# Tagging all routed rows with one copy, and SyncE's order written out in a mixture-of-experts layer

## The chip, the cores and the metric

The kernel runs on one core of a Trainium2 chip. The metric is the time of one execution on the device in microseconds (us); of the kernel before there are three runs.

## The reference

Attention over clusters, a dense layer, and a noisy top-2 mixture of eight experts, on 2 x 768 = 1536 tokens of 512 numbers. All is fp32. The last part, which the change is in:

```python
logits = x @ w_gate                                   # 1536 x 8
noisy_logits = logits + np.log1p(np.exp(x @ w_noise)) * noise
top2 = np.argpartition(-noisy_logits, 2, axis=1)[:, :2]
top2_w = softmax(noisy_logits at top2)
for e in range(8):
    for k in range(2):
        mask = top2[:, k] == e
        h = np.maximum(x[mask] @ w1[e], 0.0)          # 512 -> 1024
        out[mask] += top2_w[mask, k, None] * (h @ w2[e])
```

The attention masks each query's scores to the keys of its own cluster; the dense layer is 512 -> 2048 -> 512 with h * sigmoid(1.702 h) between.

## The kernel before

Every fp32 product is made of three matmuls of a high and a low part (hi x hi, hi x lo, lo x hi), so weights and activations exist as pairs: ACT casts the high part (`weights_hi`, `hh`, `xT` at index 0), DVE or POOL subtracts the low one (`weights_lo`, `hl`, `xT` at index 1).

The program has three stretches. Attention lasts to about 440 us. The dense layer works on the two batches b = 0 and b = 1 in turn; between its steps a hook routes b = 0 and starts loading the first expert. `middle` (576 to 632 us) routes b = 1 beside the first halves of experts 0 and 1; its instructions stand in order of a table of times, WIN, and the engines keep that order. `moe2` runs what is left, and `rest` holds loops for tokens beyond the capacities.

**Routing.** For each batch the 768 tokens stand in NB = 6 row blocks of 128 tokens, 512 numbers and 4 tag numbers each (R, ROW = 516). DVE works out each token's two experts, weights and slots. `route_scatter(R, j)` copies the tags of block j into R (L1041) and sends the block's rows to its two slots in the DRAM tensor xs, by two indirect DMAs of POOL (L1043): twelve per batch. `route_end` (L1050 and on), after b = 1 only, ranks experts 2 to 7 by their number of tokens, largest first (`rank`, result ord and ordi), and fills a small table tab for `rest` (`table`), with nr, the number of rounds.

**The experts.** Experts 0 and 1 take 480 rows each, in two halves of 240 (`gather_half`, tile Xh; the second half needs b = 1's scatters). The other six follow in order of size with capacities CAPS of 108 x 4, 104 x 4, 102 x 4, 100 x 4, 98 x 4 and 128 x 3 rows; slot e below is the e-th expert in that order, from 2 to 7. `gather(e)` loads a slot's rows as tile X (L1158). Xh and X share one buffer (tag R of the pool `rows`), so a gather must wait until PE has transposed the whole of the tile before. PE transposes 128 columns at a time (`xpose_part`, L1229) into xT, then runs FFN1 in eight blocks fb (L1325) and FFN2 (L1348 for the halves, L1378 for the slots). After each FFN1 block ACT makes hh (L1333) and DVE hl (L1334).

**Weights.** An expert's weights come in eight parts of 512 KB, in the order ORDER = (0, 4, 1, 5, 2, 6, 3, 7), by SP's DMA queue into staging tiles (`weights_load`, L1117 and L1119), cast by ACT (L1126), with the low part by DVE or POOL (L1130). Even experts use the tiles wA and wg, odd ones wB and wx, so one expert's weights load while the other's are in use.

In `moe2`, `load(e)` issues for slot e a register load of the expert's number from ordi, the eight parts and then the gather; `turn(e)` transposes; `load(e + 1)` stands ahead of slot e's FFN in the program. The order of each engine in `moe2` is made by a scheduler from the dependencies and its own estimate of times; the program's order is only its input. SP's queue and ACT's and PE's instructions so stand in an order that the code doesn't show.

Of the kernel before, what the change touches and what calls it, by code (L numbers as in the profile page):

```python
# [8 lines left out]
F32 = mybir.dt.float32  # L9
# [604 lines left out]
class Moe:  # L614
# [38 lines left out]

    def init_piece(self, i):
# [383 lines left out]

    def route_scatter(self, R, j):
        nc = self.nc  # L1040
        nc.vector.tensor_copy(R[j][:, DM:ROW], self.rmeta[:, j, :])  # L1041
# [8 lines left out]
    def route_end(self):  # L1050
        v, end = self.nc.vector, self.rtot[:, NB, 0:2]
        over = self.rtile("over", 2)
        v.tensor_scalar(over, end, float(-MAIN), 0.0, op0=OP.add, op1=OP.max)
        v.scalar_tensor_tensor(end, over, float(MAIN), self.over[:, 0], op0=OP.add, op1=OP.add)
        self.rank(self.rtot[:, NB, :])
        self.table(self.rtot[:, NB, :])

    def rank(self, total):

        c, v, n = self.const, self.nc.vector, E - 2  # L1060
        key, pos = c.tile([128, n], F32, name="key"), c.tile([128, n], F32, name="rpl")
        big = self.rtile("big", n, n)
        self.ord, self.cap = c.tile([128, n], F32, name="ord"), c.tile([128, E], F32, name="cap")
        self.ordi = c.tile([128, n], I32, name="ordi")
        v.scalar_tensor_tensor(key, total[:, 2:], float(E), self.ie[:, 2:], op0=OP.mult, op1=OP.subtract)
        row = lambda a: a[:, None, :].to_broadcast([128, n, n])
        col = lambda a: a.rearrange("p (n o) -> p n o", o=1).to_broadcast([128, n, n])
        v.tensor_tensor(big, row(key), col(key), op=OP.is_gt)
        v.tensor_reduce(pos.rearrange("p (n o) -> p n o", o=1), big, axis=AX.X, op=OP.add)
        v.tensor_tensor(big, row(pos), col(self.ie[:, :n]), op=OP.is_equal)  # L1070
        at = self.rtile("at", n, n)
        v.tensor_tensor(at, big, row(self.ie[:, 2:]), op=OP.mult)
        v.tensor_reduce(self.ord.rearrange("p (n o) -> p n o", o=1), at, axis=AX.X, op=OP.add)
        v.tensor_copy(self.ordi, self.ord)
        caps = c.tile([128, n], F32, name="caps")
        for r, (cp, ck) in enumerate(CAPS):
            v.memset(caps[:, r:r + 1], float(cp * ck))
        v.tensor_tensor(at, big, col(caps), op=OP.mult)
        v.memset(self.cap[:, :2], float(CAP))
        v.tensor_reduce(self.cap[:, 2:].rearrange("p (n o) -> p n o", o=1), at.rearrange("p r n -> p n r"),  # L1080
                        axis=AX.X, op=OP.add)

    def table(self, total):
        nc, v = self.nc, self.nc.vector
        tb = self.const.tile([128, ROUNDS, E, 4], F32, name="tb")
        v.memset(tb, 0.0)
        for r in range(1, ROUNDS):
            o = BASE + CMIN + (r - 1) * CAP
            v.tensor_scalar_add(tb[:, r, :, 0], total, float(-o))
            v.tensor_scalar(tb[:, r, :, 1], self.ie, float(REG), float(o), op0=OP.mult, op1=OP.add)  # L1090
            v.tensor_copy(tb[:, r, :, 2], self.ie)
        v.tensor_scalar_add(tb[:, 1, :, 3], self.cap, float(-CMIN))
        nc.sync.dma_start(self.tab.rearrange("(o r) n -> o (r n)", o=1), tb[0:1].rearrange("p r e n -> p (r e n)"))
        mx = self.const.tile([128, 1 + ROUNDS], F32, name="mx")
# [54 lines left out]
    def weights(self, e, par):  # L1149
        we = [w[bass.ds(e, 1)].rearrange("o k n -> (o k) n") for w in (self.w1, self.w2)]  # L1150
        W = [None] * 8
        for s in ORDER:
            W[s] = self.weights_part(e, par, s, we)
# [416 lines left out]
```

## Time and profile before

| | us |
|---|---|
| runs before | 936.96, 939.82, 941.28 |
| median of them | 939.82 |
| profiled execution | 941.51 |
| its span | 939.6 |

The span is the time from the first to the last instruction in the trace of the profiled execution; 1.9 us of its time lie around it. Positions below count from the span's start. TensorE's granted clock was 0.972 of the full clock over the span. A page line gives an engine's busy time, its share of the span and its number of instructions; a timeline line gives start, length, engine, line and operation, output <- inputs, and in brackets for how long the engine had been idle before it and what released it. SPq is the DMA queue of SP.

### The profile page before, as it was taken

Reading aid. Unit: us, or ns where it says so; the run is one execution under the profiler, and the core shown is the slowest. Engines: PE = TensorE matmul, PEld = TensorE weight load, DVE = VectorE, ACT = ScalarE, POOL = GpSimd, SP = SyncE. Lnnn points to the kernel's source line nnn. Section 1 sums busy time; section 2 is a strip of 40 time slices with the busy share of each in tenths; the row PEclk is TensorE's granted clock in tenths of the full one; section 3 lists DMA queues with packets and bytes.
Section 4 is the critical chain, followed back from the end, with each engine's and each line's share of the span. In section 5 each row is a group of like instructions: output and inputs, shape, how many; then the busy total and the mean of one; then the engine's idle time right before and its main releaser. Section 6 shows DMA issues by size and latency. Waiting matters only on the chain. (4 is left out here: it accounts for less than half of the span.)

```text
span 939.6 us, 14934 instructions
## 1 busy us (share of the span) xinstructions
PE 887.8 (94%) x5277; PEld 812.0 (86%) x5277; DVE 592.7 (63%) x1190; ACT 489.6 (52%) x1021; POOL 374.8 (40%) x398
## 2 busy tenths in 40 slices
PE   6999999999898999999999999899999899999993
PEld 4898989899887888888998979888889799999992
DVE  3889898998884667675447643836564445555231
ACT  2788888888794556554445433414444243432210
POOL 3134443454455988880000601562341334342121
PEclk8999999999898999999999999899999899999997
DMA  8756675677331344311111331274774737552120
GB/s 212 192 145 184 165 202 137 177 186 206 110 127 33 111 135 119 118 42 61 44 28 32 144 88 46 90 243 121 242 208 117 182 109 210 171 178 68 33 66 35
DMA packets 77532, 120.14 MB, mean 128 GB/s; under 512 B 9858, under 2 KB 55939, under 8 KB 76941
## 3 DMA queue, kind: packets, MB, share of 16 engines
q1 hardware_dynamic: 69997, 100.98, 37.5%
q0 software_dynamic: 7456, 18.16, 6.1%
q8 instruction: 43, 0.70, 0.3%
q14 instruction: 36, 0.29, 0.1%
HBM read 72.85 MB, written 23.76 MB: 103 GB/s over the span
## 5 line engine op out<-in xcount | busy, mean ns | idle before, releaser
L434 DVE TENSOR_TENSOR PTl<-ps_pt,PTh 128x384 fp32r<-128x384 f32 x192 | 98.8, 549 | 11.5 <-ACT PTh L429 10.4
L429 ACT ACTIVATE PTh<-ps_pt 128x384 fp32r<-128x384 f32 x192 | 87.9, 497 | 29.1 <-PE ps_pt L419 28.0
L402 DVE TENSOR_REDUCE nm<-ps_s 128x1 f32<-128x768 f32 x96 | 91.2, 950 | 15.1 <-PE ps_s L397 14.8
L419 PE MATMUL ps_pt<-ident,P 128*128 128x128 f32 x576 | 88.2, 277 | 3.8 <-DVE PTl L434 3.5
L410 ACT ACTIVATE P<-ps_s,nm 128x768 f32<-128x768 f32 x96 | 87.3, 910 | 4.9 <-DVE nm L402 4.9
L1333 ACT ACTIVATE hh<-bank 128x240 fp32r<-128x240 f32 (+6 forms) x80 | 35.2, 446 | 90.7 <-PE bank L1325 84.7
L1325 PE MATMUL bank<-xT,wB 128*128 128x240 f32 (+3 forms) x480 | 82.1, 319 | 0.0
L419 PEld LDWEIGHTS ps_pt<-ident,P 128*128 128x128 f32 x576 | 68.4, 141 | 13.8 <-DVE PTl L434 10.8
L1325 PEld LDWEIGHTS bank<-xT,wB 128*128 128x128 f32 x480 | 76.7, 189 | 2.5 <-DVE hl L1334 0.3
L1130 POOL TENSOR_TENSOR wA<-stg,wA 128x512 fp32r<-128x512 f32 x16 | 20.7, 1296 | 139.1 <-DVE wol L714 66.7
L822 PE MATMUL bank<-woh,gh 128*128 128x512 f32 x192 | 76.2, 397 | 0.0
L822 PE MATMUL bank<-wol,gh 128*128 128x512 f32 x192 | 75.0, 391 | 0.0
L1334 DVE SCALAR_TENSOR_TENSOR hl<-bank,hh 128x240 fp32r<-128x240 f32 (+6 forms) x80 | 40.2, 505 | 49.0 <-ACT hh L1333 48.2
L396 PE MATMUL ps_s<-k,q 128*128 128x384 f32 x192 | 70.7, 368 | 0.4 <-ACT P L410 0.2
L822 PE MATMUL bank<-woh,gl 128*128 128x512 f32 x192 | 70.7, 391 | 0.0
L397 PE MATMUL ps_s<-k,q 80*128 80x384 f32 x192 | 66.3, 346 | 2.6 <-DMA q<-ohT 2.6
L1363 POOL DMA_INDIRECT out_dram<-Y,idx x31 | 33.2, 1071 | 77.3 <-DVE Y L1362 68.5
L1126 ACT ACTIVATE wA<-stg 128x512 fp32r<-128x512 f32 x52 | 32.5, 632 | 43.5 <-DMA stg<-in_moe_w_dram 15.6
L454 PE MATMUL ps_o<-PTl,vs 128*128 128x256 f32 x288 | 54.0, 296 | 0.0
L454 PE MATMUL ps_o<-PTh,vs 128*128 128x256 f32 x288 | 53.7, 295 | 0.3 <-ACT T L461 0.2
L1325 PE MATMUL bank<-xT,wA 128*128 128x240 f32 (+3 forms) x300 | 53.2, 328 | 0.0
L1325 PEld LDWEIGHTS bank<-xT,wA 128*128 128x128 f32 x300 | 49.6, 197 | 1.3
(311 smaller groups left out, 2322.6 us busy)
## 6 DMA issues: line engine op xcount, KB each, us to landing
stg<-in_moe_w_dram SPq DMA_DIRECT2D x64, 512.0 KB
q<-ABq SPq DMA_DIRECT2D x48, 192.0 KB
k<-ABk SPq DMA_DIRECT2D x48, 192.0 KB
si<-in_moe_w_in_dram SPq DMA_DIRECT2D x14, 512.0 KB
so<-in_moe_w_out_dram SPq DMA_DIRECT2D x14, 512.0 KB
xs<-zrow SPq DMA_DIRECT2D x24, 217.7 KB
ld<-in_k_dram SPq DMA_DIRECT2D x8, 384.0 KB
ld<-in_q_dram SPq DMA_DIRECT2D x8, 384.0 KB
```

What stands on the lines that cost most here:

```text
L396: self.nc.tensor.matmul(o, self.g("S1", u, "q")[:, h, qs], self.g("S1", u, "k")[:, h, ks], start=True, stop=False)
L397: self.nc.tensor.matmul(o, self.g("S2", u, "q")[:80, h, qs], self.g("S2", u, "k")[:80, h, ks], start=False, stop=True)
L402: self.nc.vector.tensor_reduce(nm, self.g("s", j)[:, :, :384], axis=AX.XY, op=OP.max, negate=True)
L410: self.nc.scalar.activation(P, self.t.pop(("s", j))[:, :, :384], AF.Exp, bias=self.t.pop(("nm", j)), scale=1.0, accum_out=self.g("sums", u ...
L419: self.nc.tensor.transpose(ps[:, k, :], P[:, k * 128:(k + 1) * 128], self.ident)
L429: self.nc.scalar.activation(self.pt_at(j, g, 0), self.g("pt", j, g), AF.Copy)
L434: self.nc.vector.tensor_sub(self.pt_at(j, g, 1), self.t.pop(("pt", j, g)), f(self.pt_at(j, g, 0)))
L454: self.nc.tensor.matmul(self.g("O", u, qp)[:, h, :], vs[:, h, 2 * i + half].rearrange("p a d -> p (a d)"), PTx[:, kc, :], start=(c == 1 an ...
L822: nc.tensor.matmul(acc[j], g[:, sl], w, start=(fb == 0 and n == 0), stop=(fb == FB1 - 1 and n == 2))
L1325: self.nc.tensor.matmul(ps, w[:, kb, :], xT[:, kb, x], start=(kb == 0 and i == 0), stop=(kb == KB - 1 and i == 2))
L1333: self.nc.scalar.activation(hh, ps, AF.Relu)
L1334: self.nc.vector.scalar_tensor_tensor(hl, ps, 0.0, f(hh), op0=OP.max, op1=OP.subtract)
```

## The change

1. The tags of all six row blocks of a batch are copied by one operation (`route_tag`) ahead of the scatters, for b = 0 in the hook and for b = 1 in `middle`. R is one tile of 128 x 6 x 516.
2. In `route_end` the constants (capacities, the table's zeros, offsets and expert numbers) are made once, by POOL at the start of the program, 22 operations; `rank` and `table` are folded into `route_end`, with fewer DVE operations, ordi sooner, and a table without the row of round 0.
3. SP's order in `moe2` is the program's, by `manual_schedule`; and in `load` the gather of a slot's rows stands behind the sixth weight part (`late` in `weights`) instead of the eighth.

```diff
@@ (constants, at the start)
+        g, n, r = nc.gpsimd, E - 2, ROUNDS - 1
+        self.caps, self.cap = c.tile([128, n], F32, name="caps"), c.tile([128, E], F32, name="cap")
+        for i, (cp, ck) in enumerate(CAPS):
+            g.memset(self.caps[:, i:i + 1], float(cp * ck))
+        g.memset(self.cap[:, :2], float(CAP))
+        self.tb, self.offs = c.tile([128, r, E, 4], F32, name="tb"), c.tile([128, r, E], F32, name="offs")
+        g.memset(self.tb, 0.0)
+        for i in range(r):
...
+            g.memset(self.offs[:, i], float(o))
+            g.tensor_scalar(self.tb[:, i, :, 1], self.ie, float(REG), float(o), op0=OP.mult, op1=OP.add)
+            g.tensor_copy(self.tb[:, i, :, 2], self.ie)
...
+    def route_tag(self, R):
+        self.nc.vector.tensor_copy(R[:, :, DM:ROW], self.rmeta)
+
     def route_scatter(self, R, j):
         nc = self.nc
-        nc.vector.tensor_copy(R[j][:, DM:ROW], self.rmeta[:, j, :])
         for i in range(2):
...
-    def weights(self, e, par):
+    def weights(self, e, par, late=lambda: None):
...
-        for s in ORDER:
+        for n, s in enumerate(ORDER):
             W[s] = self.weights_part(e, par, s, we)
+            if n == 5:
+                late()
...
@@ middle
+        at("sc", did("sr", lambda: self.route_tag(self.R), "rm"), -0.01)
...
@@ moe2, load
-            n["W"] = self.weights(i, e % 2)
-            n["X"] = self.gather(i, *CAPS[e - 2])
+            n["W"] = self.weights(i, e % 2, lambda: n.__setitem__("X", self.gather(i, *CAPS[e - 2])))
...
@@ the hook, b = 0
+            moe.route_tag(Rb[0])
             for j in range(NB):
                 moe.route_scatter(R0, j)
...
-    moe.moe2(s["W"], W1, *s["A"][1][1:])
+    with tc.manual_schedule(engines={mybir.EngineType.SP}):
+        moe.moe2(s["W"], W1, *s["A"][1][1:])
     moe.rest()
```

Where the instructions move. In the lists, L1119 and L1117 of the kernel before are L1116 and L1114 of the changed one, L1166 and L1158 are L1165 and L1157, L1229 is L1228, L1130 is L1127, L1043 is L1060.

POOL at the scatters of b = 1, before:

```order
L1043 DMA xs<-R_7091,rridx 13824x516 x10
L1130 TENSOR_TENSOR wB_7587<-stg_7580,wB_7586 128x512
L1130 TENSOR_TENSOR wx_7577<-stg_7590,wx_7577 128x512
L1043 DMA xs<-R_7091,rridx 13824x516 x2
L1363 DMA out_dram<-Y,idx 1536x512 x2
```

and now:

```order
L1060 DMA xs<-R_7109,rridx 13824x516 x12
L1127 TENSOR_TENSOR wB_7577<-stg_7570,wB_7576 128x512
L1127 TENSOR_TENSOR wx_7567<-stg_7580,wx_7567 128x512
L1363 DMA out_dram<-Y,idx 1536x512 x2
L1209 DMA Y<-out_dram,idx 120x512 x2
```

The last two scatters stood behind two subtractions for weight parts, and now stand ahead of them.

SP's queue around the second halves' gather (Xh), before:

```order
L1433 ISA x2
L1433 TENSOR_LOAD ordi
L1433 ISA x2
L1455 TENSOR_LOAD nr
L1455 ISA x2
L1119 ISA
L1119 DMA stg_8072<-in_moe_w_dram 128x2x512
L1117 ISA
L1117 DMA stg_8082<-in_moe_w_dram 128x4x256
L1166 DMA Xh<-xs 120x1032 x2
L1119 ISA
L1119 DMA stg_8090<-in_moe_w_dram 128x2x512
```

and now:

```order
L1092 DMA tab<-tb 1x96
L1454 TENSOR_LOAD nr
L1454 ISA x2
L1165 DMA Xh<-xs 120x1032 x2
L1433 TENSOR_LOAD ordi
L1433 ISA x2
L1114 ISA
L1114 DMA stg_8056<-in_moe_w_dram 128x4x256
L1116 ISA
L1116 DMA stg_8064<-in_moe_w_dram 128x2x512
```

Three weight parts of slot 2 (stg_8064, further up, stg_8072 and stg_8082) and six register loads stood ahead of Xh; now the table and nr alone do, and the parts follow.

SP's queue around slot 2's gather (X, 108 x 4 rows), before, from the seventh part on:

```order
L1117 ISA
L1117 DMA stg_8120<-in_moe_w_dram 128x4x256
L1119 ISA
L1119 DMA stg_8130<-in_moe_w_dram 128x2x512
L1158 ISA
L1158 DMA X<-xs 108x2064
L1117 ISA
L1117 DMA stg_8391<-in_moe_w_dram 128x4x256
```

and now, from the fifth part on:

```order
L1114 ISA
L1114 DMA stg_8092<-in_moe_w_dram 128x4x256
L1116 ISA
L1116 DMA stg_8102<-in_moe_w_dram 128x2x512
L1157 ISA
L1157 DMA X<-xs 108x2064
L1114 ISA
L1114 DMA stg_8114<-in_moe_w_dram 128x4x256
L1116 ISA
L1116 DMA stg_8124<-in_moe_w_dram 128x2x512
```

The gather stood behind the eighth part and now stands behind the sixth; the same holds for every slot.

PE at the first transpositions of Xh, before:

```order
L1325 MATMUL bank_7755<-xT_6781,wB_7586 128x240 x2
L1325 MATMUL bank_7755<-xT_6781,wB_7587 128x240
L1348 MATMUL bank_7596<-wx_7577,hl_7729 120x512
L1348 MATMUL bank_7597<-wx_7577,hl_7729 120x512
L1348 MATMUL bank_7596<-wx_7577,hh_7751 120x512 x2
L1348 MATMUL bank_7597<-wx_7577,hh_7751 120x512 x2
L1229 MATMUL bank_7806<-ident,Xh 128x120 x2
L1348 MATMUL bank_7596<-wx_7577,hl_7752 120x512
```

and now:

```order
L1325 MATMUL bank_7730<-xT_6799,wB_7572 128x240 x2
L1325 MATMUL bank_7730<-xT_6799,wB_7573 128x240
L1228 MATMUL bank_7798<-ident,Xh 128x120 x2
L1228 MATMUL bank_7803<-ident,Xh 128x120
L1348 MATMUL bank_7588<-wx_7567,hh_7720 120x512 x2
L1325 MATMUL bank_7747<-xT_6799,wB_7576 128x240 x2
L1325 MATMUL bank_7747<-xT_6799,wB_7577 128x240
L1325 MATMUL bank_7747<-xT_6799,wB_7576 128x240 x2
```

The first transpositions of Xh stood behind FFN1 of block 7 and FFN2 of blocks 5 and 6 (the latter's hl part excepted); now three of them stand ahead of all that, right behind FFN1 of block 6.

PE at the first transpositions of slot 2's X, before:

```order
L1325 MATMUL bank_8161<-xT_7797,wB_7184 128x240 x2
L1325 MATMUL bank_8161<-xT_7797,wB_7185 128x240
L1325 MATMUL bank_8161<-xT_7797,wB_7184 128x240 x2
L1325 MATMUL bank_8161<-xT_7797,wB_7185 128x240
L1229 MATMUL bank_8332<-ident,X 128x108 x4
L1229 MATMUL bank_8339<-ident,X 128x108
L1325 MATMUL bank_8192<-xT_7797,wB_7358 128x240 x2
```

and now:

```order
L1348 MATMUL bank_7831<-wA_6891,hh_7955 120x512
L1348 MATMUL bank_7832<-wA_6890,hh_7955 120x512
L1348 MATMUL bank_7832<-wA_6891,hh_7955 120x512
L1228 MATMUL bank_8324<-ident,X 128x108 x4
L1228 MATMUL bank_8331<-ident,X 128x108 x3
L1325 MATMUL bank_7982<-xT_7780,wA_6322 128x240 x2
L1325 MATMUL bank_7982<-xT_7780,wA_6323 128x240
```

They stood behind the second FFN1 block of expert 1's second half (wB), and now stand ahead of the last FFN1 block of expert 0's second half (wA), three FFN1 blocks sooner. The first eight transpositions of the 104 x 4 rows move ahead likewise, the last eight do not.

## Rows read from the trace of the kernel before

**Rows 1.** The page, part 1: busy us (share of the span) xinstructions of each engine
```profile
PE 887.8 (94%) x5277; PEld 812.0 (86%) x5277; DVE 592.7 (63%) x1190; ACT 489.6 (52%) x1021; POOL 374.8 (40%) x398
```

**Rows 2.** PE's timeline: start us, us, engine line operation, count [idle before <-releaser]
```profile
550.09 0.44 PE L729 MATMUL bank<-xh,wih 128*128 128x384 f32 x1 [1.25 <-DVE xT L1232]
...
600.97 0.22 PE L993 MATMUL bank<-rrM,tri 128*128 128x48 bf16 x1 [2.38 <-DVE rrM L943]
...
635.34 0.66 PE L1229 MATMUL bank<-ident,Xh 120*128 120x120 f32 x2 [2.88 <-DMA Xh<-xs]
...
692.76 0.55 PE L1229 MATMUL bank<-ident,X 104*128 104x104 f32 x4 [0.90 <-DMA X<-xs]
...
742.14 2.10 PE L1378 MATMUL bank<-hh,wB 128*128 128x416 f32 x5 [3.92 <-ACT hh L1333]
```

**Rows 3.** The windows: us, busy time of each engine, PEclk, DMA share, GB/s
```profile
550.00:552.00 2.00, 1.91 (x11) 1.92 (x12) 1.63 (x4) 0.00 (x0) 0.00 (x0) 1.00 0.52 162
601.00:605.00 4.00, 4.00 (x19) 3.74 (x20) 3.69 (x24) 0.99 (x3) 1.28 (x1) 0.58 0.77 254
635.00:639.00 4.00, 3.66 (x12) 2.95 (x13) 1.86 (x9) 0.74 (x2) 1.07 (x1) 0.57 0.68 167
742.00:748.00 6.00, 5.86 (x18) 5.50 (x19) 4.97 (x12) 2.38 (x5) 2.46 (x2) 0.52 0.48 159
```

**Rows 4.** POOL's timeline at the start of the program and in the routing of b=1
```profile
41.22 1.01 POOL L341 TENSOR_TENSOR sc<-eq,rev 128x384 f32<-128x384 f32 x1 [27.06 <-DVE eq L335]
...
608.79 0.98 POOL L1043 DMA_INDIRECT xs<-R,rridx  x1 [1.06 <-DVE R L1041]
...
620.36 0.96 POOL L1043 DMA_INDIRECT xs<-R,rridx  x1 [0.30 <-issue]
621.35 1.29 POOL L1130 TENSOR_TENSOR wB<-stg,wB 128x512 fp32r<-128x512 f32 x1
...
625.32 0.97 POOL L1043 DMA_INDIRECT xs<-R,rridx  x1 [0.30 <-issue]
```

**Rows 5.** The DMA issues of 606 to 630 us: median us from issue to landing
```profile
xs<-R,rridx POOLq DMA_INDIRECT x12, 3.9
```

**Rows 6.** DVE's timeline: the tag copy of the last row block
```profile
616.50 0.16 DVE L1041 COPY R<-rmeta 128x4 f32<-128x4 f32 x1
```

**Rows 7.** SP's timeline, DMA issues of 620 to 730 us
```profile
631.03 0.81 SPq L1166 DMA_DIRECT2D Xh<-xs  x2
...
650.81 0.37 SPq L1119 DMA_DIRECT2D stg<-in_moe_w_dram  x1
...
657.75 0.33 SPq L1158 DMA_DIRECT2D X<-xs  x1
...
676.36 0.37 SPq L1119 DMA_DIRECT2D stg<-in_moe_w_dram  x1
...
684.60 0.34 SPq L1158 DMA_DIRECT2D X<-xs  x1
...
727.04 0.29 SPq L1158 DMA_DIRECT2D X<-xs  x1
727.59 0.37 SPq L1117 DMA_DIRECT2D stg<-in_moe_w_dram  x1
```

**Rows 8.** PE's timeline where PE's order changes
```profile
628.65 1.08 PE L1348 MATMUL bank<-wx,hh 128*120 128x512 f32 x4
...
651.57 1.09 PE L1348 MATMUL bank<-wA,hh 128*120 128x512 f32 x4
...
658.36 1.51 PE L1325 MATMUL bank<-xT,wA 128*128 128x240 f32 x12
...
788.63 1.27 PE L1378 MATMUL bank<-hh,wA 128*128 128x408 f32 x6
```

**Rows 9.** ACT's timeline, the start of experts' FFN1 in ranks 2 and 3
```profile
740.53 1.15 ACT L1126 ACTIVATE wB<-stg 128x512 fp32r<-128x512 f32 x2 [7.96 <-DMA stg<-in_moe_w_dram]
...
782.06 1.15 ACT L1126 ACTIVATE wg<-stg 128x512 fp32r<-128x512 f32 x2 [3.33 <-DMA stg<-in_moe_w_dram]
```

More of the change, by code (lines that the diff above doesn't have):

```diff
@@ L652, in consts @@
         self.zrow = z
+        g, n, r = nc.gpsimd, E - 2, ROUNDS - 1
[6 more added lines that the diff above has]
+        for i in range(r):
+            o = BASE + CMIN + i * CAP
+            g.memset(self.offs[:, i], float(o))
+            g.tensor_scalar(self.tb[:, i, :, 1], self.ie, float(REG), float(o), op0=OP.mult, op1=OP.add)
+            g.tensor_copy(self.tb[:, i, :, 2], self.ie)
+        self.mx = c.tile([128, 1 + ROUNDS], F32, name="mx")
+        g.memset(self.mx[:, 1:2], 1.0)
     def init_piece(self, i):
@@ L1050, in route_end @@
     def route_end(self):
-        v, end = self.nc.vector, self.rtot[:, NB, 0:2]
+        nc, c, v, n = self.nc, self.const, self.nc.vector, E - 2
+        total, end = self.rtot[:, NB, :], self.rtot[:, NB, 0:2]
+        row = lambda a: a[:, None, :].to_broadcast([128, n, n])
+        col = lambda a: a.rearrange("p (n o) -> p n o", o=1).to_broadcast([128, n, n])
+        key, pos = self.rtile("key", n), self.rtile("rpl", n)
+        big, at = self.rtile("big", n, n), self.rtile("at", n, n)
+        self.ord, self.ordi = c.tile([128, n], F32, name="ord"), c.tile([128, n], I32, name="ordi")
+        v.scalar_tensor_tensor(key, total[:, 2:], float(E), self.ie[:, 2:], op0=OP.mult, op1=OP.subtract)
+        v.tensor_tensor(big, row(key), col(key), op=OP.is_gt)
+        v.tensor_reduce(pos.rearrange("p (n o) -> p n o", o=1), big, axis=AX.X, op=OP.add)
+        v.tensor_tensor(big, row(pos), col(self.ie[:, :n]), op=OP.is_equal)
+        v.tensor_tensor(at, big, row(self.ie[:, 2:]), op=OP.mult)
+        v.tensor_reduce(self.ord.rearrange("p (n o) -> p n o", o=1), at, axis=AX.X, op=OP.add)
+        v.tensor_copy(self.ordi, self.ord)
+        v.tensor_tensor(at, big, col(self.caps), op=OP.mult)
+        v.tensor_reduce(self.cap[:, 2:].rearrange("p (n o) -> p n o", o=1), at.rearrange("p r n -> p n r"),
+                        axis=AX.X, op=OP.add)
         over = self.rtile("over", 2)
@@ L1054, in route_end @@
         v.scalar_tensor_tensor(end, over, float(MAIN), self.over[:, 0], op0=OP.add, op1=OP.add)
[L1055 to L1094, printed above, removed]
-        left = self.const.tile([128, E], F32, name="left")
+        v.tensor_tensor(self.tb[:, :, :, 0], total[:, None, :].to_broadcast([128, ROUNDS - 1, E]), self.offs,
+                        op=OP.subtract)
@@ L1096, in table @@
+        v.tensor_scalar_add(self.tb[:, 0, :, 3], self.cap, float(-CMIN))
+        nc.sync.dma_start(self.tab.rearrange("(o r) n -> o (r n)", o=1),
+                          self.tb[0:1].rearrange("p r e n -> p (r e n)"))
+        left, mx = self.rtile("left", E), self.mx
         v.scalar_tensor_tensor(left, self.cap, float(BASE), total, op0=OP.add, op1=OP.is_lt)
@@ L1098, in table @@
         v.tensor_reduce(mx[:, 0:1], left, axis=AX.X, op=OP.max)
-        v.memset(mx[:, 1:2], 1.0)
-        for r in range(1, ROUNDS):
-            v.tensor_single_scalar(mx[:, r + 1:r + 2], mx[:, 0:1], float(BASE + CMIN + (r - 1) * CAP), op=OP.is_gt)
+        v.tensor_tensor(mx[:, 2:], mx[:, 0:1].to_broadcast([128, ROUNDS - 1]), self.offs[:, :, 0], op=OP.is_gt)
         self.nr = self.const.tile([128, 1], I32, name="nr")
@@ L1187, in gather_rest @@
         t = self.cs.tile([CP, 4], F32, tag="t", name="t")
-        nc.sync.dma_start(t, self.tab[bass.ds(r * E + e, 1)].to_broadcast([CP, 4]))
+        nc.sync.dma_start(t, self.tab[bass.ds((r - 1) * E + e, 1)].to_broadcast([CP, 4]))
         sl = self.cs.tile([CP, CK, 4], F32, tag="sl", name="sl")
@@ L1473 @@
     xs = dram.tile([E * REG, ROW], F32, name="xs")
-    tab = dram.tile([ROUNDS * E, 4], F32, name="tab")
+    tab = dram.tile([(ROUNDS - 1) * E, 4], F32, name="tab")
     ident = const.tile([128, 128], F32, name="ident")
@@ L1501 @@
     R0 = [moe.row(0, acc, j) for j in range(NB)]
+    Rb = [moe.R]
     b0ctx.close()
```

## The prediction

> **What bounds the kernel.** I read the page's busy times first. PE is busy 94% of the span, no other engine more than 63% [rows 1], so a microsecond counts only if PE idles in it or runs at the low clock in it. Then PE's timeline after the attention, for the places where it idles: 1.25 us at 550, 2.38 at 601, 2.88 at 635, 0.90 at 693, 3.92 at 742 [rows 2]. Then the windows behind these stops, for the clock. Behind 1.25 us the granted clock stays at 1.00. Behind 2.38 us it is 0.58 for four microseconds, behind 2.88 it is 0.57, behind 3.92 it is 0.52 for six [rows 3]: about the lower of the two levels, 1.2 of 2.4 GHz. So a long stop costs more than itself: 4 x (1 - 0.57) = 1.7 us behind the stop at 635, 6 x (1 - 0.52) = 2.9 us behind that at 742. A fall sets in somewhere between 1.25 and 2.38 us of idle time. Last come POOL's, SP's and ACT's timelines, for who releases these stops, and the order of the changed program, for what PE will ask for sooner.
>
> **The tag copies.** Of the six copies the last comes at 616.50 [rows 6], long after the first scatter at 608.79, because the whole end of the routing stands before it on DVE. Scatters follow each other every (620.36 - 608.79) / 9 = 1.285 us; the eleventh and twelfth stand behind two casts' subtractions of 1.29 us each, and the twelfth starts at 625.32 [rows 4]. With all twelve in a row the last starts at 620.36 + 2 x 1.285 = 622.9, so 2.4 us sooner. The two subtractions then run from 623.9 to 626.5. PE wants the first of them for the FFN1 block behind the row at 628.65 [rows 8], so they stay covered, and the indirect writes behind them start no later, since POOL's work up to there is the same. Five DVE copies of 0.16 us fewer touch nothing PE waits for.
>
> **The constants.** 22 operations go from DVE's routing to POOL's start. Priced like the small copy, 0.16 us, they are 3.5 us of POOL. POOL is idle for 27.06 us before its work at 41.22 [rows 4]: cost nothing. If that cover were gone, 3.5 us at the start is the bound. The shorter routing end on DVE is off PE's path.
>
> **SP's order, first step: Xh.** The gather Xh waits for all twelve scatters. It went out at 631.03, 5.7 us after the last scatter's start, and landed when PE's transposition could start at 635.34: 4.3 us [rows 2, 4, 7]. In the change no weight load lies beside the last scatters, so I take less than their median landing of 3.9 us [rows 5]: 3.3. Xh goes out at 622.9 + 3.3 = 626.2 and lands at 630.5. But the changed order also puts PE's first transpositions of Xh ahead of the work from 628.65 on; formerly PE ran on until 635.34 - 2.88 = 632.46. It now stops 3.81 us of work sooner, and the gain is (635.34 - 3.81) - 630.5 = **1.0 us**, not the 4.8 by which the gather is earlier. Its stop becomes 630.5 - 628.65 = 1.9 us, between the idle time that kept the clock and the one that lost it; I let the clock fall as before. Ends: a 5.7 us landing of the scatter as before costs 2.4 us against this, so a loss of 1.4; a stop short enough for the clock gives 1.7 more, so a gain of 2.7. The three weight parts that went out before Xh now follow it. Even with the 8.2 us of the slow gather below they land near 637, and the sixth part, which waits for staging buffers that they free, went out only at 650.81 [rows 7]: cost nothing.
>
> **Second step: X of the first routed expert of the last six (108 x 4 rows).** Its gather stood behind parts 7 and 8 and went out at 657.75. Behind part 6, at 650.81, it needs only that the last transposition of Xh has freed its buffer. That now stands before the row at 651.57, so it goes out at about 652.1 [rows 7, 8]. The neighbour, 104 x 4 rows, took 692.76 - 684.60 = 8.2 us to land [rows 2, 7]. That gives 660.2. PE's changed order asks for it at 658.36, ahead of an FFN1 block and three FFN1 blocks sooner than it did [rows 8]. New stop: 660.2 - 658.4 = 1.8 us; all times here shift together, so the first step does not change it. Between a landing of 7 us, since parts 7 and 8 no longer go first, and one of 8.5, it is 0.6 to 2.1. I take **+1.8** and no fall of the clock; a fall would add 1.7. The Trainium skill (DMA: Bandwidth & Descriptors, "Why a DMA increments its semaphore by 16 and not by 1") says that a transfer uses the largest number of engines, up to 16, that divides its slowest dimensions: 13 for 104 rows, 12 for 108. By that the landing would be 8.2 x (108/12) / (104/13) = 9.2 us, the stop 2.8, and the sum 1.0 us higher. The trace agrees in kind: 102 rows, six engines by that rule, give the slowest gather of all, with the part behind it landing after 12.9 us [rows 7, 9]; no row shows the 108-row tile's landing.
>
> **Third step: X of 104 x 4 rows.** Behind part 6 it goes out at about 676.9 instead of 684.60 [rows 7] and lands at 685. The stop of 0.90 us at 692.76 goes [rows 2]: **-0.9**. It can't give more, since that stop was no longer; it can give less if the tile, whose first transpositions move ahead too, comes late there.
>
> **Fourth step: X of 102 x 4 rows.** It waits at 727.04 for PE's last transpositions of the 104-row tile [rows 7], which stay where they were. The part behind it, 727.59, is what ACT waits 7.96 us for, until 740.53, with the activation that PE stands for behind it [rows 2, 9]. Now part 7 of the same expert stands there instead of part 1 of the next, and ACT's order again puts its two casts ahead of that activation. **0**; the 3.92 us and the 2.9 of clock stay.
>
> **Fifth step: X of 100 x 4 rows.** ACT's order now puts the cast of the following expert's second part ahead of the activation that PE wants at 788.63 [rows 8]. That part's staging buffer comes free when a subtraction of 1.29 us behind the casts that end at 782.06 + 1.15 has run [rows 4, 9], at about 784.5. With 4.3 us for the load as for Xh, half of 1.15 for the cast, and 742.14 - 741.68 = 0.5 for the activation until PE goes on, PE goes on at 789.9, 1.3 late. I take **+1.0**, ends 0 (a load in 3.0) and 1.9 (one in 4.9). The last two gathers and the end of the kernel are covered as before.
>
> **Sum.** -1.0 + 1.8 - 0.9 + 0 + 1.0 = +0.9 us, on the profiled execution's 941.51: 942.4. That execution lay 1.69 above the median of the runs, 939.82, so against the median I forecast **940.7 us**: no change that a measurement tells, since about 0.5% (4.7 us) is what one can tell here.
>
> **Rivals.** *The big stop goes* (chance 0.11). If the 102-row gather or what stands behind it came in time, 3.92 + 2.9 = 6.8 us would go: 940.7 - 6.8 = 933.9. For it: gathers do go out sooner elsewhere. Against: this one is held by PE's transpositions, not by SP. *Both early stops close* (0.14). The stop for Xh stays short of the fall (-2.7) and the 108-row gather lands in 6.3 us without a stop, with the 0.9 gained and none at 788: -3.6, so 936.2. For it: less traffic beside both. Against: the 8.2 us of its neighbour. *Asked for too soon* (0.20). PE's order asks at 658.36 and 788.63 for data that lands 1.8 to 1.9 us later, and each time the clock falls: (1.8 + 1.7) + (1.9 + 1.7) - 0.9 - 1.0 = +5.2 on the median, 945.0, slower. It decides where a stop passes the point between 1.25 and 2.38 us [rows 2, 3]. *The change does not do what it says* (0.05): if Xh goes out no sooner, because scatters in a row land slower, PE stops for 6.7 us at 628.65, 3.8 us are lost there instead of 1.0 won, and the time is 940.7 + 4.8 = 945.5. My forecast has 0.50.
>
> **Range.** The forecast's own ends: -2.7 + 0.6 - 0.9 + 0 = -3.0 and +1.4 + 2.1 + 1.7 - 0.9 + 1.9 = +6.2, so 936.8 to 946.0. For 8 times in 10 I go down to **934.0**, nearly to the rival without the big stop, and up to **946.5**, past the slow one. Faster by over 0.5%, below 935.1: the first rival and part of the second, 0.18. Slower, above 944.5: most of the third and of the fourth, 0.18. Within: 0.64.
>
> **What would show it.** Twelve scatters in one row, the last at 622.9; Xh out near 626.2; PE's stop for it about 1.9 us, with or without a low clock behind it. A new stop of PE for the 108-row tile of 1 to 2 us near 657; none near 692; one of 3.9 near 742 with ACT waiting for a weight load, and a small one near 788. It is wrong if PE's stop near 742 is gone, if the stop for the 108-row tile is over 3 us, or if a stop appears that none of these steps names.

## The result, and the profile after

The changed kernel takes 951.04 us (median of four runs, 950.09 to 957.92), the kernel before 940.04 in the same session (936.96 to 941.28): a ratio of 1.0141, with a 95% interval of 1.0115 to 1.0167. (The ratios on record, here and below, are not the quotients of the medians; that quotient is 1.0117 here.) The change makes it slower, and 951.0 lies outside the range of the prediction. The profiled execution of the changed kernel took 950.09 us (span 948.3, mean granted clock 0.975); the one of before took 941.51 (span 939.6, 0.972). So 8.7 us are to be found between the two traces, and 11.0 between the medians.

The page's first part for the changed kernel, which answers to [rows 1]:

```profile
PE 886.0 (93%) x5277; PEld 807.1 (85%) x5277; DVE 596.8 (63%) x1161; ACT 490.8 (52%) x1021; POOL 377.6 (40%) x416
```

PE does the same work in nearly the same busy time: 886.0 against 887.8 us. The rest of the span, 62.3 us against 51.8, is time in which PE idles, and it has grown by 10.5. Next come PE's waits from 600 to 940 us, first of the kernel before, then of the changed one (line, what was waited for: us in total, times, longest):

```profile
PE bank L1378 <- ACT hh L1333: 4.7, 2, 3.9
PE bank L1229 <- DMA Xh<-xs: 2.9, 1, 2.9
PE bank L993 <- DVE rrM L943: 2.4, 1, 2.4
PE bank L1229 <- DMA X<-xs: 0.9, 1, 0.9
```

```profile
PE bank L1378 <- ACT hh L1333: 5.7, 4, 2.9
PE bank L1378 <- DVE hl L1334: 3.9, 2, 2.6
PE bank L1228 <- DMA Xh<-xs: 2.8, 1, 2.8
PE bank L1228 <- DMA X<-xs: 2.6, 2, 1.4
PE bank L1008 <- DVE rrM L958: 2.4, 1, 2.4
PE bank L1348 <- DVE hl L1334: 1.9, 1, 1.9
```

Two rows have no counterpart before: PE waits for DVE's `hl`, once in the halves (L1348) and twice in the slots (L1378). The sums, 10.9 and 19.3 us, differ by 8.4 of those 10.5; the other 2 lie ahead of 600 us. No step of the prediction named a stop for `hl`.

PE's timeline says where; these are the stops of over 0.5 us from 620 on, which answer to [rows 2]:

```profile
631.21 0.53 PE L1228 MATMUL bank<-ident,Xh 120*128 120x120 f32 x3 [2.82 <-DMA Xh<-xs]
...
654.58 0.72 PE L1348 MATMUL bank<-wA,hl 128*120 128x512 f32 x2 [1.93 <-DVE hl L1334]
...
663.02 0.84 PE L1228 MATMUL bank<-ident,X 108*128 108x108 f32 x7 [1.15 <-DMA X<-xs]
...
689.88 0.64 PE L1228 MATMUL bank<-ident,X 104*128 104x104 f32 x5 [1.43 <-DMA X<-xs]
...
745.91 1.21 PE L1378 MATMUL bank<-hh,wB 128*128 128x416 f32 x5 [2.94 <-ACT hh L1333]
...
751.79 1.40 PE L1378 MATMUL bank<-hh,wx 128*128 128x416 f32 x6 [1.03 <-ACT hh L1333]
...
760.21 1.02 PE L1378 MATMUL bank<-hl,wx 128*128 128x416 f32 x4 [1.26 <-DVE hl L1334]
...
794.18 1.00 PE L1378 MATMUL bank<-hh,wA 128*128 128x408 f32 x4 [0.92 <-ACT hh L1333]
...
803.71 1.00 PE L1378 MATMUL bank<-hl,wA 128*128 128x408 f32 x4 [2.60 <-DVE hl L1334]
...
841.14 1.00 PE L1378 MATMUL bank<-hh,wx 128*128 128x400 f32 x4 [0.80 <-ACT hh L1333]
```

To see which of these cost anything, I paired the k-th `hh` activation of ACT in both traces. The changed kernel is 0.4 us ahead at 628, level at 642, 3.9 behind at 655 to 659, 4.4 behind at 699, still 4.7 at 737 and 4.1 at 768, 7.6 behind at 825 and 8.6 at the end. So there are two steps: about +4.7 by 700, of which 3.9 stand by 659, and about +4 between 785 and 845. Between single blocks the difference swings by some microseconds, since the blocks' order has changed too. The stretch around 742 costs neither kernel clearly more than the other.

**The first step.** The windows of the changed kernel behind the stops at 631, 654 and 742 (columns as in [rows 3]: the length, the busy time of PE, PEld, DVE, ACT and POOL, then the granted clock, the DMA share and GB/s):

```profile
631.00:635.00 4.00, 3.67 (x17) 3.23 (x18) 1.64 (x8) 0.37 (x1) 0.00 (x0) 0.64 1.04 328
655.00:660.00 5.00, 5.00 (x25) 4.35 (x24) 1.98 (x5) 2.23 (x5) 1.01 (x1) 0.66 0.84 269
742.00:748.00 6.00, 3.06 (x18) 2.62 (x17) 1.85 (x3) 2.02 (x4) 2.25 (x2) 1.00 0.51 153
```

The stop at 654 is followed by a clock of 0.66 for five microseconds, 5 x 0.34 = 1.7 us more. With its own 1.93 that is 3.6 of the 3.9 by which the kernel falls back there. DVE's timeline shows what `hl` waited behind, POOL's what that waited for; the changed kernel's rows:

```profile
645.66 1.45 POOL L1363 DMA_INDIRECT out_dram<-Y,idx  x1 [0.30 <-DVE m L1179]
...
652.74 0.17 DVE L1181 CAST idx<-Xh 120x2 int32<-120x2 f32 x1 [5.54 <-DMA out_dram<-Y,idx]
```

and those of the kernel before:

```profile
641.48 1.02 POOL L1363 DMA_INDIRECT out_dram<-Y,idx  x1 [0.30 <-DVE xT L1232]
...
644.72 0.17 DVE L1182 CAST idx<-Xh 120x2 int32<-120x2 f32 x1 [0.68 <-DMA out_dram<-Y,idx]
```

The small cast of `idx` writes into one of two buffers, and must wait until the output write that read that buffer has landed. DVE's queue is held for 5.54 us by it instead of 0.68: the write goes out 4.2 us later, and takes 652.74 - 645.66 = 7.1 us to land instead of 3.2. Behind the cast on DVE stand the low parts of wA, and with them the staging buffers that SP needs for the fifth weight part. SP's timeline, the gathers and the fifth part (L1114):

```profile
626.44 0.81 SPq L1165 DMA_DIRECT2D Xh<-xs  x2
...
654.24 0.37 SPq L1114 DMA_DIRECT2D stg<-in_moe_w_dram  x1
...
655.51 0.36 SPq L1157 DMA_DIRECT2D X<-xs  x1
...
680.33 0.37 SPq L1157 DMA_DIRECT2D X<-xs  x1
...
731.70 0.32 SPq L1157 DMA_DIRECT2D X<-xs  x1
```

So the gather behind the sixth part is held by DVE, not by the transposition that the prediction named, and goes out at 655.51 instead of 652.1.

**The second step.** DVE's timeline around 803:

```profile
801.39 1.76 DVE L1207 MEMSET Y<- 102x2048 f32 x1 [2.97 <-DMA out_dram<-Y,idx]
803.07 0.10 DVE L1181 CAST idx<-X 100x4 int32<-100x4 f32 x1
803.09 0.57 DVE L1334 SCALAR_TENSOR_TENSOR hl<-bank,hh 128x408 fp32r<-128x408 f32 x1
```

The clearing of the next output tile waits 2.97 us for an output write, and PE's `hl` stands right behind it: the stop of 2.60 us at 803.71. The stop of 1.26 at 760 has the same form. The engines' orders have moved with the gather; and SP stands still for it. SP's waits at the slots' gathers from 640 to 870 us, before and now:

```profile
SPq L1158 <- PE bank L1229: 30.1, 3, 12.8
...
SPq L1158 <- PE bank L1378: 11.2, 1, 11.2
```

```profile
SPq L1157 <- PE bank L1378: 52.4, 3, 19.4
...
SPq L1157 <- PE bank L1228: 17.8, 1, 17.8
...
SPq L1157 <- DVE idx L1181: 8.0, 4, 3.1
```

That is 41.3 us before and 78.2 now. A gather two parts earlier in SP's queue does not start two parts earlier, since its tile has one buffer: that of the 102 x 4 rows went out at 727.04 [rows 7] and now does at 731.70, in a kernel that is 4.7 us behind there. It holds the seventh and eighth part back while it waits for it. ACT's waits for weight parts from 600 to 900 us rise from 48.1 to 62.1 us in all; the row that grows, before and now:

```profile
ACT wA L1126 <- DMA stg<-in_moe_w_dram: 15.6, 6, 5.7
```

```profile
ACT wA L1123 <- DMA stg<-in_moe_w_dram: 30.2, 11, 7.0
```

Those are two traces beside each other; what the edit's parts cost is for the experiments.

### The profile page after: what moved, and what is told of

Read it like the earlier page. It is cut to its first block, busy times and chain, and to the rows that moved or that the text cites. A ratio compares the mean times of both kernels' runs of the same rounds, so it can differ in the third digit from the quotient of the medians.

```text
span 948.3 us, 14908 instructions
## 1 busy us (share of the span) xinstructions
PE 886.0 (93%) x5277; PEld 807.1 (85%) x5277; DVE 596.8 (63%) x1161; ACT 490.8 (52%) x1021; POOL 377.6 (40%) x416
## 5 line engine op out<-in xcount | busy, mean ns | idle before, releaser
L1127 POOL TENSOR_TENSOR wA<-stg,wA 128x512 fp32r<-128x512 f32 x16 | 21.0, 1312 | 126.7 <-DVE wol L729 66.7
L454 PE MATMUL ps_o<-PTh,vs 128*128 128x256 f32 x288 | 53.7, 295 | 0.3 <-ACT T L461 0.2
```

What stands on the lines that cost most here:

```text
L454: self.nc.tensor.matmul(self.g("O", u, qp)[:, h, :], vs[:, h, 2 * i + half].rearrange("p a d -> p (a d)"), PTx[:, kc, :], start=(c == 1 an ...
```

## The experiments

The changed kernel has three parts: the tags with the routing's constants, the order of SP, and the place of the gather. Each run below has its ratio to the kernel before of its own session, with the 95% interval, since the kernel before itself stood between 939.1 and 945.2 us from session to session.

### One part at a time

e1_tags, the changed kernel without the last two parts:

```diff
-            if n == 5:
+            if n == 7:
-    with tc.manual_schedule(engines={mybir.EngineType.SP}):
-        moe.moe2(s["W"], W1, *s["A"][1][1:])
+    moe.moe2(s["W"], W1, *s["A"][1][1:])
```

> The tag copy, the constants and the shorter end of the routing alone; SP's order is the scheduler's again and the gather stands behind the eighth part. My theory: the 11 us come from the orders that the earlier gather makes on DVE and PE (the cast of idx and the clearing of Y stand ahead of work PE needs and wait there for indirect writes to land). Then this is within 2 us of the kernel before, so 938 to 942, and PE's stop for Xh near 635 gets shorter, since the last scatter is 2.4 us sooner. Rival 1 (SP's order is the cost, its loads being late): also 938 to 942. Rival 2 (the routing's edit is the cost, by its changed DVE order): 945 or more.

Measured: 941.85 us, 1.0022 (1.0002 to 1.0042). The gather Xh goes out at 625.04, 6 us sooner than before, but PE's order asks for it sooner as well, and its stop is 3.72 us. SP stands at the slots' gathers for 41.4 us. The tags, the constants and the routing's shorter end bring nothing together and cost 0.2%, if anything. I had expected a shorter stop for Xh. ACT waits 54.2 us for parts here, with no loss to speak of.

e2_sp_only, the kernel before with the other two parts:

```diff
-            n["W"] = self.weights(i, e % 2)
-            n["X"] = self.gather(i, *CAPS[e - 2])
+            n["W"] = self.weights(i, e % 2, lambda: n.__setitem__("X", self.gather(i, *CAPS[e - 2])))
+    with tc.manual_schedule(engines={mybir.EngineType.SP}):
+        moe.moe2(s["W"], W1, *s["A"][1][1:])
```

> SP's program order and the gather behind the sixth part, on the kernel before; the tags are copied six times. My theory and rival 1: 948 to 953, with DVE's wait for a landed output write near 650 and PE's stop behind it. Rival 2 (the routing's edit): within 2 us of 940.

Measured: 947.43, 1.0071 (1.0038 to 1.0104): half of the loss without any of the tags, and just under the 948 that I had expected at least. SP stands at the gathers for 77.9 us, ACT waits 63.9 us for parts. DVE's wait at the `idx` cast is 1.9 us here and 1.35 in e1, against 5.54 with all three parts.

e3_sp_gather8, the changed kernel with the gather back behind the eighth part:

```diff
-            if n == 5:
+            if n == 7:
```

> All of the change but one number: the gather stands behind the eighth part, SP's order stays the program's. My theory: the orders of DVE and PE are nearly those of before, the cast of idx waits less than 1 us, no stop at 654; 938 to 942. Rival 1 (SP's order, with three weight parts behind Xh, is the cost): 947 to 952.

Measured: 944.03, 1.0026 (1.0004 to 1.0049). One number in the code takes most of the loss back, if not down to the 942 that I had expected at most. Its SP waits at the gathers:

```profile
SPq L1157 <- PE bank L1228: 29.6, 3, 12.2
...
SPq L1157 <- PE bank L1378: 10.9, 1, 10.9
```

40.5 us, as before the change, and ACT's 53.7 us for parts lie nearer to the 48.1 than to the 62.1. There is no stop at 760 or 803: the second step belongs to the gather's place. The wait of 5.5 us for `idx` and the stop of 1.94 at 654 are still there, so the first step's local cause does not: it comes with the tags and SP's order together. (Its profiled execution, 947.33, is the slowest of its six runs. It falls back by 6.0 us between 626 and the end, where the changed kernel's falls back by 9.1, so this one trace alone would show less of a return than the times do.)

e4_no_sp_order, the changed kernel without the prescribed order of SP, the gather behind the sixth part:

```diff
-    with tc.manual_schedule(engines={mybir.EngineType.SP}):
-        moe.moe2(s["W"], W1, *s["A"][1][1:])
+    moe.moe2(s["W"], W1, *s["A"][1][1:])
```

> All of the change but SP's order, which is the scheduler's again, with the gather behind the sixth part in the program. If the scheduler keeps weight parts ahead of Xh and the idx cast waits little, the first stretch costs at most 2 us and the later stops are there: 943 to 947 by theory A. If the gather's place alone is the whole cost (theory C), 949 to 952.

Measured: 950.29, 1.0117 (1.0072 to 1.0163). SP stands at the gathers for 77.6 us, ACT for parts 64.1. The wait at the `idx` cast is 2.28 here and PE's stop for `hl` in the halves is gone, and still the loss is whole. (Its profiled execution, 945.73, is the fastest of its four runs: it comes to 626 us 4.7 ahead of the kernel before and ends 4.3 behind, so it loses 9.0 in this stretch.) With e1 and e3 this closes the square: behind the eighth part 1.0022 and 1.0026, behind the sixth 1.0117 and 1.0141, each time without and with SP's order. The quotients of the medians, 1.0022, 1.0045, 1.0099 and 1.0117, say the same with a smaller step. **Shown: with the tags in the kernel, about 1% of the 1.4% comes with the gather's place. Prescribing SP's order costs nothing that can be told.** How much the place costs depends on the rest: e2 has the same place and the same order of SP without the tags, and loses 0.7% where the whole change loses 1.4%, with intervals that do not meet. The gather's place alone, in the kernel before, was not run.

### Which slots

e9_first2 puts the gather behind the sixth part for slots 2 and 3 alone, e10_last4 for slots 4 to 7 alone:

```diff
-            if n == 5:
+            if n == at:
...
-            n["W"] = self.weights(i, e % 2, lambda: ...)
+            n["W"] = self.weights(i, e % 2, lambda: ..., 5 if e < 4 else 7)   # e10: 7 if e < 4 else 5
```

> The change, but the gather stands behind the sixth part for slots 2 and 3 alone; slots 4 to 7 have it behind the eighth, as before. Theory A (two separate causes: SP's program order around 630 to 700, worth some 4 to 6 us, and the orders that the earlier gather makes in slots 3 to 5, worth some 4 us more): the shift against before at 785 stays until the end, no stop on hl near 803 of over 1 us; 944 to 948. Theory B (the later stops only follow from the lateness of the first stretch): 950 to 952, like the whole change.

> The change, but the gather stands behind the sixth part for slots 4 to 7 alone. Theory A: the first stretch is as in the run with the eighth part (PE stops at 654 behind DVE), and the stops near 760 and 803 on hl are there; 946 to 951. Theory B: no different from the run with the eighth part, 942 to 945.

Measured: 952.26, 1.0135 (1.0101 to 1.0169), and 952.13, 1.0116 (1.0084 to 1.0149). Either half of the move costs as much as the whole. The two steps of the traces are therefore not two prices that add up, and both expectations are missed. In e10 SP stands at the gathers for 81.3 us and PE has one stop of 7.8 us for `hh`. In e9 it is 42.4 us, as before the change, though ACT's wait for parts is 61.6; its profile is the fastest of its four runs. (It comes to 626 us 3.8 ahead of the kernel before and ends 5.0 behind, so it loses 8.8 there.) SP's time at the gathers alone does not settle e9.

### The cast that waits for an output write

e5_idx4 gives `idx` four buffers in the changed kernel, e21_sp8_idx4 in e3:

```diff
+        self.ix = self.pool(ctx, "c_i", 4, side="right")
...
-        idx = self.cs.tile([cp, ck, 1], I32, tag="idx", name="idx")
+        idx = self.ix.tile([cp, ck, 1], I32, tag="idx", name="idx")
```

> The change with four buffers for the tile idx in place of two, so that its cast needs no earlier output write to have landed. My theory: DVE's wait of 5.5 us at 647 to 653 goes, with PE's stop of 1.9 us and the low clock behind it, and the gather of 108 x 4 rows goes out some 3 us sooner: the shift against before at slot 2 falls from +4.7 to between 0 and +2, the time to 946 to 948.5. Rival 1: DVE's wait goes and PE stops as long for the loads; 950 to 952.

> The change with the gather behind the eighth part and four buffers for idx. It tests the first stretch alone: DVE's wait of 5.5 us for an output write, in front of subtractions and hl, costs the run without the four buffers (944.0) a stop of 1.9 us at 654 and the low clock behind it. If that is the cost, 939 to 942 and no stop at 654; if SP's order is late by itself (three parts behind Xh), 943 to 946.

Measured: 952.69, 1.0107 (1.0074 to 1.0139), and 951.58, 1.0129 (1.0091 to 1.0166). Both lie above what I had expected. In both the wait is gone and the stop at 654 with it, which bears out the cause read from the trace. In e21 the kernel is 0.2 us ahead of the one before at 655, where e3 is 3.9 behind. But it is no gain in the whole: other stops come, because with other buffers the scheduler writes other orders. In e21 the largest, in PE's timeline:

```profile
742.61 1.10 PE L1417 MATMUL bank<-ident,yT 128*108 128x128 f32 x4 [6.46 <-DVE Y L1363]
```

What share of the 11 us the cast has in the changed kernel stays open: neither run removes it alone. e5 shows one thing more. Its gather of 108 x 4 rows goes out at 650.80, without the hold-up by DVE, and PE still waits for it:

```profile
660.50 0.84 PE L1229 MATMUL bank<-ident,X 108*128 108x108 f32 x7 [3.33 <-DMA X<-xs]
```

9.7 us of landing, where the prediction's sum took 8.2 and the rule of the Trainium skill (DMA: Bandwidth & Descriptors, "Why a DMA increments its semaphore by 16 and not by 1") gave 9.2 as an estimate. In the changed kernel itself it landed 663.02 - 655.51 = 7.5 us after it went out, so the two measurements lie on both sides of either value.

### Does PE ask too soon?

The gather's place also moves PE's transpositions ahead. To hold that fixed, PE's order was made the program's: e15_before_pe_order (kernel before), e16_tags_pe_order (e1) and e14_sp_pe_order (changed kernel); e17_tags_pe_gpool is e16 with all gathers of slots on POOL's queue.

```diff
-    with tc.manual_schedule(engines={mybir.EngineType.SP}):
+    with tc.manual_schedule(engines={mybir.EngineType.SP, mybir.EngineType.PE}):   # e14
```

> The whole change with PE's order in the last layer also the program's: the transpositions of a gathered tile then stand in the middle of the tail of FFN2, not ahead of FFN1 blocks of the expert before. Theory D (the cost is that the scheduler's orders ask for gathered tiles, and for what hangs on them, before they land): PE's stops on Xh and X shrink from 5.8 us in all to under 2, and the time falls to 936 to 944. Theory E (the loads themselves are too late whatever PE asks first): 949 or more, the stops only move to hh and hl.

> The kernel before with PE's program order in the last layer and nothing else. It tells what that order is worth by itself: 937 to 943 by theory D, since few tiles were asked for too soon there (2.9 and 0.9 us of stops on gathers); if it is 934 or less, the two runs beside it owe their time to PE's order alone and not to the change.

> The tags and the routing's end alone (SP's order the scheduler's, gather behind the eighth part) with PE's program order in the last layer. Theory D: the earlier gather of Xh is no longer spent, 934 to 940. Theory E: 941 to 945.

> As the run with the tags and PE's program order, with the gathers of slots 2 to 7 on POOL's DMA queue, so that no weight part queues behind a gather that waits. If both the too early asking and the queue behind the gather are the costs, this beats both kernels: 928 to 935. If POOL's waits hold up its subtractions: 938 or more.

Measured: e14 989.46, 1.0500 (1.0466 to 1.0534); e15 974.36, 1.0310 (1.0266 to 1.0354); e16 976.87, 1.0364 (1.0331 to 1.0397); e17 969.89, 1.0282 (1.0234 to 1.0330). PE's program order costs some 30 us by itself. None of the four came near what Theory D expected. What counts is e14 against e16, which differ in SP's order and the gather's place while PE's order is that of the program in both (only buffer numbers differ): 12.6 us, as large as the whole loss. So a loss of this size does not need PE asking for tiles sooner. SP's waits at the gathers, e14 and then e16:

```profile
SPq L1157 <- PE bank L1228: 71.7, 5, 20.3
```

```profile
SPq L1157 <- PE bank L1228: 41.4, 5, 11.8
```

ACT waits 66.3 us for parts in e14 and 57.2 in e16. Of PE's own waits the one that grows most is for DVE's Y (L1362), 18.8 us against 12.2, so DVE's order, which the scheduler makes anew, has its part here too. e17 takes the gathers off SP's queue and gains 7.0 us on e16.

### The gathers off SP's queue

If the loss is what stands behind a waiting gather on SP, it must vanish when the gathers wait on another queue. e11_before_gather_pool does this in the kernel before, e12_after_gather_pool in the changed one:

```diff
-        self.nc.sync.dma_start(X, self.xs[...])
+        self.nc.gpsimd.dma_start(X, self.xs[...])
...
-            i = self.nc.values_load(self.ordi[0:1, e - 2:e - 1], engines=(mybir.EngineType.SP,), ...)
+            i = self.nc.values_load(self.ordi[0:1, e - 2:e - 1], engines=(mybir.EngineType.SP, mybir.EngineType.Pool), ...)
```

> The kernel before with the gathers of slots 2 to 7 on POOL's DMA queue instead of SP's. It tests the reading of the stop at 742: weight parts stand on SP's queue behind a gather that waits for PE's transpositions. If so, ACT's wait of 8.0 us and PE's stop of 3.9 us with the low clock behind it go, 933 to 937. If the parts are late for another reason, 938 to 942; if POOL's wait for the transpositions holds up its subtractions or the indirect writes, 942 or more.

> The whole change with the gathers of slots 2 to 7 on POOL's DMA queue. Theory F (behind the sixth part, SP's queue stands at a gather for 78 us in all against 41, and the weight parts behind it come late: ACT waits 62 us for weight parts against 48): with the gathers off SP's queue ACT's wait for weight parts falls to 40 to 50 us and the time to 940 to 946, like the kernel before with its gathers on POOL (943.6). If the place of the gather costs by the orders that it makes on PE and DVE, 948 to 953.

Measured: 943.64, 1.0017 (0.9992 to 1.0041), and 942.34, 1.0036 (1.0006 to 1.0065). On POOL's queue the early place costs 0.2%, within both intervals; on SP's it was 1.0%. So the loss goes with the gather standing ahead of weight parts on SP's queue. Two things change with the queue besides: the orders that the scheduler makes, and how the tile itself lands (see the last section). These runs do not part them from SP's standing still. ACT's wait in e12, 54.1 us, fell less than I had expected. In e11 the big stop of before at 742 is gone, worth 7.0 us there (6.0 us behind before at 732, 1.0 ahead at 759), but that is lost again, before it and after it: PE waits 2.9 us for `hh` at 657 and 3.36 for the tile of 104 x 4 rows, where the kernel before waits 0.9, and 2.14 for `hh` at 808 and 1.48 for `hl` at 842, where it waits 0.76 and nothing.

That suggested moving only the gather that holds the 742 stop, slot 4's, of 102 x 4 rows (e19_before_gpool_slot4), or slots 4 to 6 (e20_before_gpool_slots4to6, `cp <= 102`, `3 < e < 7`):

```diff
-        self.nc.sync.dma_start(X, ...)
+        (self.nc.gpsimd if cp == 102 else self.nc.sync).dma_start(X, ...)
...
-            ... engines=(mybir.EngineType.SP,), ...
+            ... engines=(mybir.EngineType.SP,) + ((mybir.EngineType.Pool,) if e == 4 else ()), ...
```

> The kernel before with the gather of slot 4 alone (102 x 4 rows) on POOL's queue. The stop at 742 goes (3.9 us and 2.9 us of clock), and the first stretch keeps nearly its order: 933 to 937. If it loses elsewhere what it wins there, as the run with all gathers on POOL did, 938 to 942.

> The kernel before with the gathers of slots 4 to 6 on POOL's queue. As the run beside it, with the smaller stop of 0.8 us at 808 gone too: 932 to 937; if POOL's waits hold up subtractions or output writes, 940 or more.

Measured: **933.10 us, 0.9931 (0.9904 to 0.9959)**, and 935.00, 0.9959 (0.9936 to 0.9981). e19 is faster than both kernels. Its issue in POOL's timeline, the landing in the DMA issues of 715 to 745 us (KB, then median us to landing), and PE's waits from 600 to 940:

```profile
725.45 0.62 POOL L1158 DMA_DIRECT2D X<-xs  x1 [5.20 <-PE bank L1229]
```

```profile
X<-xs POOLq DMA_DIRECT2D x1, 822.4 KB, 6.5
```

```profile
PE bank L1229 <- DMA Xh<-xs: 2.4, 1, 2.4
PE bank L1229 <- DMA X<-xs: 2.1, 1, 2.1
PE bank L1378 <- ACT hh L1333: 0.4, 1, 0.4
PE bank L1378 <- DVE hl L1334: 0.3, 1, 0.3
```

The 3.9 us for `hh` at 742 are gone. The shift against the kernel before goes from -1.9 us at 721 to -9.1 at 746: 7.2 gained, where the prediction had put 3.92 + 2.9 = 6.8 on this stop and its clock.

Last, the same one gather in e1 (e22_tags_gpool_slot4) and in the changed kernel (e23_after_gpool_slot4):

> The tags, constants and the shorter end of the routing (SP's order the scheduler's, gather behind the eighth part) with slot 4's gather on POOL's queue. If the tags cost what their run alone showed (2 us), 934 to 937, a little above the kernel before with the same edit (933.1); if the earlier gather of Xh is worth something once the stop at 742 is gone, 929 to 932.

> The whole change with slot 4's gather alone on POOL's queue. SP stood at that gather for 17.8 us with parts 7 and 8 of slot 4 behind it. If parts queued behind waiting gathers are the cost, the stop near 746 goes and those at 752 and 760 with it (2.9 + 1.0 + 1.3 us), later gathers still hold the queue: 943 to 948. If the gather's place costs by orders of PE and DVE, 949 or more.

Measured: e22 938.45, 0.9932 (0.9911 to 0.9953), where the kernel before took 945.23; e23 955.47, 1.0112 (1.0039 to 1.0185). The ratio of e22 is that of e19: the tags neither add to the gain nor take from it. e23 missed: one gather off SP leaves 57.6 us of SP waiting at the others, and the loss stays. Its profiled execution also holds a stop of ACT of 8.11 us before 626 whose releaser the trace does not show, so I read no more from it. The traces of e14, e15 and e22 have such stops near there too, of 7.27, 10.01 and 7.54 us; the others have none.

**What stays open.** The loss follows the place of the gather on SP's queue, by e1, e3, e4, e14, e16 and e12. By what path is argued from traces and not shown: how the 11 us split between SP standing still and the orders that the scheduler makes from the new place is not settled: e9 loses as much with 42 us of SP's waiting as the whole with 78, e9 and e10 do not add, and e21 loses 1.3% with the gather behind the eighth part and SP standing at the gathers for 39.4 us, so other orders alone can cost as much.

## Why the prediction was wrong

By its own steps, with the changed kernel's trace:

- **The tag copies and the constants** came as said. The constants run on POOL from 14.72 to 16.8 us, inside its idle time. The twelve scatters stand in a row, the last at 622.73 (622.9 predicted); PE is untouched by the rest.
- **Xh** went out at 626.44 (626.2 predicted) and landed by 631.21 instead of 630.5: a stop of 2.82 us, not 1.9, with a clock of 0.64 behind it. Instead of 1.0 us gained, the kernel lost the 0.4 by which it was ahead. That lies within the bounds given, a loss of 1.4; the step was off in size alone.
- **X of 108 x 4 rows** is the step that failed first. I had it go out at 652.1, "it needs only that the last transposition of Xh has freed its buffer". It went out at 655.51, since the fifth part ahead of it went out at 654.24 (sixth at 654.87), held by DVE, held by the cast of `idx`. PE stopped for `hl` (1.93) and for X (1.15), and the clock fell for 1.7 more: 4.8 us, where 1.8 was taken, 2.1 was the upper end, and 3.8 that with a fall. DVE's order had not been walked: I looked at what the moved DMAs do to PE and SP, and left out the engine between them.
- **X of 104 x 4 rows**: out at 680.33 and landed 9.55 us later, stop 1.43. I had priced its landing at some 8 us from its row in the kernel before, and called the stop gone; it grew by 0.5 instead of giving 0.9.
- **X of 102 x 4 rows**: net about 0, as predicted, but by luck, from other parts: 2.94 us without a fall of the clock, then 1.03 and 1.26, in place of 3.92 with one.
- **X of 100 x 4 rows**: the stop of 1.0 predicted near 788 is there in size, 0.92 at 794. A cast does stand ahead of the activation, but it waits for PE and not for a load, as ACT's timeline has it:

```profile
793.10 0.63 ACT L1123 ACTIVATE wA<-stg 128x512 fp32r<-128x512 f32 x1 [1.90 <-PE bank L1325]
793.63 0.49 ACT L1333 ACTIVATE hh<-bank 128x408 fp32r<-128x408 f32 x1
```

- **What no step named**: the stops for `hl`, 1.93 at 654, 1.26 at 760 and 2.60 at 803, and 0.80 for `hh` at 841. A stop that no step names was the prediction's own sign of being wrong.

Behind the steps stands a term put at nothing: that the parts which now follow a gather are covered. I worked it out for Xh ("cost nothing") and for one activation behind the 102-row tile ("0"), and left the parts behind the other gathers out. With the change ACT waits 62.1 us for parts instead of 48.1, and SP stands at the gathers for 78.2 us instead of 41.3. I priced each gather by the stop of PE for its own tile. The square of e1, e3, e4 and the change says that most of the loss hangs on the gather's place, and e12 that it hangs on SP's queue. Whether it is what stands behind the gather there, or the orders that follow from its place, stays open.

Of the rivals, *asked for too soon* gave 945.0 and the right sign, but not the mechanism that carries the loss: PE's stops for gathered tiles grew only from 3.8 to 5.4 us, and e14 against e16 loses 12.6 us with PE asking in the same order. *The big stop goes* did not happen in the change, but its price of 6.8 us was right: e19 gained 7.2 there.

## What to carry to other kernels

In this kernel a DMA moved ahead in SP's queue started earlier only where its buffer was free by then; otherwise it started nearly when it did, and what stood behind it waited with it. So price the instructions behind the moved one first, and walk the order of every engine that frees a buffer for them, not only of the one that asks for the data. Where a load waits long for a buffer and others stand behind it, try another queue for that one load: here one gather moved to POOL was worth 0.7%, three of them 0.4%, and all of them nothing.

## What the runs showed of the hardware

- The same tile of 102 x 4 rows landed in 6.5 us on POOL's queue (e19). On SP's, in the kernel before, the weight part behind it landed 12.9 us after its issue [rows 7, 9]. The Trainium skill (DMA: Bandwidth & Descriptors, "Why a DMA increments its semaphore by 16 and not by 1") sets six engines for such a tile on SP, and says that some direct copies issued by software spread over all sixteen. The traces agree for this tile. Its 102 packets of 8256 bytes are spread over 727.95 to 738.35 us on SP's queue in the kernel before, with at most 8 of them under way at a time, and over 726.77 to 731.15 on POOL's in e19, with up to 17. POOL's queue is not faster for every tile: that of 104 x 4 rows, thirteen engines by the same rule, landed there in 8.6 us (e12) and 8.7 (e11), against 8.2 and 9.55 on SP's.
- An indirect output write of 120 rows took 7.1 us to land at 645 in the changed kernel, and 3.2 at 641 in the one before.
- A stop's length alone does not tell the clock. The prediction put the fall between 1.25 and 2.38 us of idle time. Here 2.82 us were followed by 0.64 and 1.93 by 0.66, but 2.94 us before 745.91 and 2.60 us before 803.71 by 1.00.
